# A power-of-two scale of V from a matmul of ones, and 26 groups of matmuls of ones ahead of the first layer product, in an attention, SoLU and bilinear kernel

## The chip, the cores and the metric

The kernel runs on one core of one Trainium2 chip. The metric is the device time of one execution in microseconds (us). Engine names: PE is TensorE (matmuls; PEld its weight loads), DVE is VectorE, ACT is ScalarE, POOL is GpSimd, SP is SyncE, whose queue issues all of the kernel's DMAs.

## The reference

Three layers follow each other. All inputs are float32 or float64 arrays made from a normal distribution.

```
# attention: q, k, v are [4, 8, 576, 64]
scores = q @ k.T / 8
mask   = heads 0..3: 0 <= i - j < 32;  heads 4..7: i >= j and i % 32 == j % 32
x      = softmax(where(mask, scores, -1e9)) @ v          # then [2304, 512]
# layer 1: w_in [512, 1024], w_out [1024, 512]
h  = x @ w_in
s  = h * softmax(h)
ln = (s - mean(s)) / sqrt(var(s) + 1e-6) * g_ln
y  = ln @ w_out
# layer 2: w_a, w_b [512, 1536], w_out2 [1536, 512]
out = ((y @ w_a) * (y @ w_b)) @ w_out2
```

Values that a half-precision matmul multiplies are split into a high and a low part, so that three products (high by high, high by low, low by high) carry the precision. Before such a split a tensor is scaled by a power of two, and the result is scaled back. For V this power comes from the largest magnitude in V; any power near it serves.

## The kernel before, in words

**The program is a list of steps.** Every piece of work is recorded with `pe(...)`, `dve(...)`, `act(...)`, `pool(...)` or `dma(...)` as a step with a key, a planned cost, and the buffers that it reads and writes. The first number of such a call is a planned cost; it only served to make the order. The order itself stands in the file as the list `ISSUE` (L60): 3261 step numbers, in which the steps are emitted. Each engine executes its own steps in that order and waits, where a step's data or buffer is not ready, with everything behind it in its queue waiting too. SP's queue issues the DMAs in the same way. Buffers come from rings of a fixed size: a new use of a buffer waits until the last use of the one before it is done.

**Attention.** The four batches are worked on one after the other (`attention`, L965 and on). In each there are four groups of two heads: two groups of strided heads (4 to 7), then two of local heads (0 to 3). `load_qk` and `load_v` fetch them. `group_T` (L600 to L618) transposes q and k with float32 matmuls against the identity (L608) into a bank of the ring `s`, and ACT copies them out. `att_tile` then makes one tile of attention: mask and scores on PE (L696, L701), the maximum, the subtraction and the sum on DVE (L719, L728, L732), the exponential on ACT (L731), the division on POOL (L768, L777), a transpose of the weights, and the product with V into the bank `x` (L798 for batch 0, L803 to L805 for the others), which ACT copies into `xT` (L825). Batch 0 is *direct*: it multiplies in float32, needs no scale of V, and transposes its weights on PE (L764). In batches 1 to 3 V and the weights are split in two half-precision parts, and the weights are transposed by a DMA (L786).

**The scale of V.** For batches 1 to 3 `pair_scale` (L622) makes one scale for the two strided groups and one for the two local ones, six in all. DVE reduces each group's V to one maximum per partition (L630), which gives two columns `am`. `pow2_scale` (L495) then finds the largest of all: PE transposes the columns (L500), DVE takes the maximum of each row (L501), PE transposes the two results into one row (L505), DVE takes the maximum again (L506), masks all but the exponent and makes a power of two and its inverse (L511 to L513), PE spreads the two numbers over all partitions by a matmul with ones (L515), and DVE multiplies in the units (L516). The scratch for this is the right part of the PSUM bank `xbank`, whose left part is the buffer `x` of the attention results; both are rings of one buffer. The same function makes one scale for w_out (`scale_wout`) and, in other banks, three in layer 2.

**Layer 1** runs beside the attention, a tile of 128 tokens at a time (`moe1`): ACT casts `xT` to `xh` (L845), DVE makes the rest `xl` (L849), and PE multiplies with the two parts of w_in in 24 products of 512 columns (L856) into `h`, a ring of one buffer of two banks. DVE, ACT and POOL make ln from it, a DMA transposes it, and `s2` multiplies with w_out (L910) into `y`. The weights come as float64 in eight loads of 512 KB for w_in (`load_win`, L454), are turned into float32 by ACT and DVE (L455, L461, L465) and split by ACT and POOL (L474, L475); the loads go through three raw buffers, so a later one waits for the conversion of an earlier one.

**Layer 2** begins when the attention is done. Its matmuls are L1326 (products with w_a and w_b) and L1472 (with w_out2). Ahead of it stands the one place where the kernel already multiplies ones by ones: `prime` (L1086) marks four banks in this way.

The constants are made at the beginning: `constants_a` the identity, `constants_b` and `constants_c` the two masks, `constants_d` (L424) the tiles of ones, `ones` in float32 and `onesb` in bfloat16, and some small ones. In `ISSUE` they stand in the order a, b, d, c on POOL.

Of the kernel before, what the change touches and what calls it, by code (L numbers as in the profile page):

```python
# [8 lines left out]
F32 = mybir.dt.float32  # L9
# [43 lines left out]
PARAM = dict(back=12, first=40, early=(0,), seed=4, noise=0.1, direct=((0, 0), (0, 1)), stay=0.0, pf1=(),  # L53
# [222 lines left out]
def tile_banded_attention_solu_bilinear(  # L276
# [19 lines left out]
    def pe(us, fn, r, w, cols=60, mode=0): return P.op("PE", us, fn, r, w, cols, mode=mode)  # L296
# [1331 lines left out]
```

## Time and profile before

| | |
|---|---|
| median of the runs | 700.77 us (3 runs, 699.4 to 700.79) |
| the profiled execution's own time | 695.03 us |
| its span, first to last instruction | 693.3 us |
| PE busy | 664.4 us (96%) |
| DVE busy | 571.5 us (82%) |
| ACT busy | 447.2 us (65%) |
| POOL busy | 144.7 us (21%) |
| mean granted clock of PE | 0.994 |
| DMA moved | 109.68 MB, mean 158 GB/s |

The profile shows a single execution. Its busy times are sums over instructions, whose ends are modelled for matmuls, and a stretch can be read as busy although its instructions only follow each other at a lower clock. The granted clock of PE is a share of full speed: 0.5 is the lower of its two levels, 1.2 GHz, and 1.0 the upper, 2.4 GHz. In a row that names a wait, the instruction on the left stood still until the one on the right was done.

### The profile page before, as it was taken

Reading aid. Unit: us, or ns where it says so; the run is one execution under the profiler, and the core shown is the slowest. Engines: PE = TensorE matmul, PEld = TensorE weight load, DVE = VectorE, ACT = ScalarE, POOL = GpSimd, SP = SyncE. Lnnn points to the kernel's source line nnn. Section 1 sums busy time; section 2 is a strip of 40 time slices with the busy share of each in tenths; the row PEclk is TensorE's granted clock in tenths of the full one; section 3 lists DMA queues with packets and bytes.
Section 4 is the critical chain, followed back from the end, with each engine's and each line's share of the span. In section 5 each row is a group of like instructions: output and inputs, shape, how many; then the busy total and the mean of one; then the engine's idle time right before and its main releaser. Section 6 shows DMA issues by size and latency. Waiting matters only on the chain.

```text
span 693.3 us, 15572 instructions
## 1 busy us (share of the span) xinstructions
PE 664.4 (96%) x5991; PEld 498.8 (72%) x5991; DVE 571.5 (82%) x1238; ACT 447.2 (65%) x898; POOL 144.7 (21%) x268
## 2 busy tenths in 40 slices
PE   5987899999999999999999999999999999999997
PEld 4766677878787888886576676766767676775676
DVE  5789899789678644999999999799977989786576
ACT  3679868777767644986978787676543746434421
POOL 5544546536537432410000000000000000000000
PEclk9999899999999999999999999999999999999999
DMA  9999979999998434677254043653522304641023
GB/s 209 258 243 244 188 138 194 264 186 268 222 248 199 102 81 102 188 249 240 103 184 152 0 141 104 198 201 97 175 100 94 120 32 166 237 138 46 1 92 122
DMA packets 152650, 109.68 MB, mean 158 GB/s; under 512 B 101376, under 2 KB 131072, under 8 KB 152576
## 3 DMA queue, kind: packets, MB, share of 16 engines
q1 hardware_dynamic: 152576, 108.69, 60.4%
q8 instruction: 47, 0.77, 0.5%
q14 instruction: 27, 0.22, 0.1%
HBM read 65.41 MB, written 27.53 MB: 134 GB/s over the span
## 4 chain that ended last, share of the span: by engine, by line
PE 61%; DVE 8%; ACT 5%; issue 1%; POOL 0%; ACTq 0%; POOLq 0%
PE N L1326 17%; PE M L1326 13%; PE N L1472 9%; PE y L910 7%; PE M L1472 7%; PE h L856 6%; ACT y L1267 1%; DVE p L1423 1%; ACT w L1128 1%; DVE w L1132 1%; DVE y L1269 1%; DVE A L1415 1%; DVE A L1393 1%; DVE V L647 0%; ACT Z L1238 0%
## 5 line engine op out<-in xcount | busy, mean ns | idle before, releaser
L1326 PEld LDWEIGHTS <-w 128*128 128x128 f16 x1512 | 147.9, 98 | 91.7 <-issue 2.0
L1326 PE MATMUL N<-y,w 128*128 128x384 f16 x864 | 156.2, 326 | 0.7 <-ACT N L1333 0.7
L1472 PEld LDWEIGHTS <-p 128*128 128x128 f16 x1071 | 104.7, 98 | 20.4 <-issue 1.1
L1326 PE MATMUL M<-y,w 128*128 128x384 f16 x648 | 118.5, 326 | 0.8 <-ACT N L1333 0.8
L910 PE MATMUL y<-lnT,wout 128*128 128x256 f16 x864 | 101.4, 273 | 1.5 <-DMA lnT<-ln 0.8
L910 PEld LDWEIGHTS <-wout 128*128 128x128 f16 x864 | 82.0, 98 | 15.2 <-issue 4.1
L1418 ACT CAST p<-A 128x384 f16<-128x384 f32 x119 | 59.2, 512 | 40.1 <-DVE A L1393 22.6
L856 PE MATMUL h<-win,xh 128*128 128x512 f32 x288 | 79.8, 417 | 2.7 <-DVE wk L871 2.6
L1472 PE MATMUL N<-wo,p 128*128 128x256 f16 x612 | 77.7, 273 | 1.0 <-DVE yst L1488 1.0
L856 PEld LDWEIGHTS h<-win,xh 128*128 128x128 f32 x288 | 54.4, 198 | 14.4 <-DVE wk L871 3.3
L1423 DVE TENSOR_TENSOR p<-A,p 128x384 f16<-128x384 f32 x119 | 62.3, 552 | 2.7 <-ACT p L1418 2.7
L1472 PE MATMUL M<-wo,p 128*128 128x256 f16 x459 | 60.2, 273 | 0.0
L455 ACT ACTIVATE f64f<-raw 128x512 f32<-128x512 f32 x52 | 34.6, 674 | 11.2 <-DMA raw<-in_moe_w_in_dram 7.3
L856 PE MATMUL h<-win,xl 128*128 128x512 f32 x144 | 39.2, 394 | 0.0
L1415 DVE TENSOR_TENSOR A<-A 128x384 f32<-128x384 f32 x72 | 39.0, 553 | 0.2
L1488 DVE SCALAR_TENSOR_TENSOR ob<-M,osc,ob 128x256 f32<-128x256 f32 x63 | 27.8, 477 | 12.6 <-PE M L1472 11.1
L777 POOL TENSOR_TENSOR e<-e,r 128x324 f32<-128x324 f32 (+2 forms) x30 | 26.2, 881 | 50.0 <-DVE r L738 28.2
L861 DVE TENSOR_REDUCE st<-h 128x1 f32<-128x1024 f32 x18 | 22.0, 1220 | 17.2 <-PE h L856 17.1
L856 PEld LDWEIGHTS h<-win,xl 128*128 128x128 f32 x144 | 26.7, 188 | 5.9
L465 DVE SCALAR_TENSOR_TENSOR f64f<-f64f,raw 128x512 int32<-128x512 int32 x36 | 28.8, 804 | 2.3 <-ACT f64f L455 1.8
L1348 ACT COPY V<-M 128x384 f32<-128x384 f32 x36 | 17.0, 473 | 20.0 <-PE M L1326 19.9
L871 DVE SCALAR_TENSOR_TENSOR wk<-h,st,wk 128x1024 f32<-128x1024 f32 x18 | 23.0, 1279 | 7.8 <-POOL st L869 7.7
(191 smaller groups left out, 1207.0 us busy)
## 6 DMA issues: line engine op xcount, KB each, us to landing
raw<-in_moe_w_out_dram SPq DMA_DIRECT2D x20, 512.0 KB
o_scr<-ob SPq DMA_DIRECT2D x36, 256.0 KB
ob<-o_scr SPq DMA_DIRECT2D x30, 256.0 KB
raw<-in_moe_w_a_dram SPq DMA_DIRECT2D x12, 512.0 KB
raw<-in_moe_w_b_dram SPq DMA_DIRECT2D x12, 512.0 KB
y_scr<-y SPq DMA_DIRECT2D x14, 384.0 KB
y<-y_scr SPq DMA_DIRECT2D x14, 384.0 KB
y_scr<-ys SPq DMA_DIRECT2D x18, 256.0 KB
```

The costliest lines, as they stand in the source:

```text
L455: act(0.67, lambda: nc.scalar.activation(f(), raw()[:, :, 1].bitcast(F32), AF.Prelu, scale=2.0 ** -112, alpha=-2.0 ** 32), (raw,), (f,))
L465: dve(0.77, lambda: nc.vector.scalar_tensor_tensor(g().bitcast(I32), f().bitcast(I32), 3, raw()[:, :, 0], op0=ALU.logical_shift_left, op1= ...
L777: pool(0.1 + 1.2 * pl, lambda: nc.gpsimd.tensor_tensor(ev(), ev(), r()[:, :ng].unsqueeze(2).to_broadcast([128, ng, nk]), op=ALU.mult), (r, ...
L856: nc.tensor.matmul(h()[:, 512 * n:512 * n + 512], xs[xa]()[:, kk], win[wa][:, kk, 512 * n:512 * n + 512], start=(pi == 0 and kk == 0), sto ...
L871: dve(1.3, lambda: nc.vector.scalar_tensor_tensor(e(), h(), st()[:, 7:8], e(), op0=ALU.mult, op1=ALU.mult, accum_out=st()[:, 2:3]), (h, (s ...
L910: nc.tensor.matmul(y()[:, 256 * mi:256 * mi + 256], wout[:, kk, wa, 128 * m:128 * m + 128], lnT()[:, xa, kk], start=(pi == 0 and kk == 0), ...
L1326: nc.tensor.matmul(to()[:, :HB], w()[:, wa, a, kk], y7[b]()[:, xa, kk], start=first and pi == 0 and kk == 0, stop=pi == 2 and kk == 1, ski ...
L1415: dve(TD, lambda: nc.vector.tensor_tensor(to(), x(), y(), op=op), toks, (to,))
L1418: act(0.5, lambda: nc.scalar.copy(pu(0, a), x()), (x,), (pu.tok(0, a),))
L1423: dve(TD, lambda: nc.vector.tensor_tensor(pu(1, a), x(), pu(0, a), op=ALU.subtract), (x, pu.tok(0, a)), (pu.tok(1, a),))
L1472: nc.tensor.matmul(bk(i), pus[u](xa, a)[:, 128 * tt:128 * tt + 128], wo()[:, u, b, wa], start=a == A11 and u == 0 and pi == 0, stop=u == U ...
L1488: dve(0.475, lambda: nc.vector.scalar_tensor_tensor(dst(), bk(i), s(), dst(), op0=ALU.mult, op1=ALU.add), (src, osc), (obt(t, c),))
```

## The change

The change has three parts. The scale of V is now made from the sum of the maxima of all partitions in place of their maximum. Two accumulating matmuls with a 128x128 tile of ones add up the columns `am` over the partitions and leave the sum on every partition at once. DVE masks the exponent, and three DVE steps make the power, its inverse and the unit. The result lies in the buffer `x`, which now is the whole bank `xbank`; the ring `scp` is gone, and the scale of w_out takes a buffer of `x` too. Next, 26 groups of eight matmuls of ones by ones (128 columns, bfloat16) are recorded, with keys from 3.5 to 38.5, which write an `h` buffer that nothing reads. They are the steps 13 to 38 of the new list, so that all later numbers shift: the first load of w_in, 181 before, is 207 now. Last, the planned costs of PE's steps are a little higher (0.05 to 0.1 for most) and the list `ISSUE` is written anew, now with 3263 numbers. In it `constants_d` (number 4 in both) is emitted first on POOL.

```
-PARAM = dict(back=12, first=40, ...
+PARAM = dict(warm=tuple(3.5 + 1.4 * i for i in range(26)), scp="x", back=12, first=40, ...
...
 ISSUE = [int(n) for n in """
-10 0 13 11 14 5 2 15 16 1 12 6 18 17 21 8 35 19 9 20 7 4 22 414 37 430 3 771 787 36 39 38 40 43 41 42 181 187 23 66 44
...
+5 4 39 0 40 13 41 11 2 1 10 42 6 14 43 44 12 207 8 15 45 9 213 7 61 219 440 452 3 789 801 63 46 62 65 16 64 66 67 17
...
-    ring("psR", "x", None, F32, 1).fixed = lambda n: xbank[:, :352]
-    ring("psR", "scp", None, F32, 1).fixed = lambda n: xbank[:, 352:]
+    ring("psR", "x", None, F32, 1).fixed = lambda n: xbank
...
-        tp = bank(ps) if ps == "M" else rings[ps].new()
+        tp = bank(ps) if ps == "M" else rings[ps or pm["scp"]].new()
...
-        pow2_scale(am, (am,), len(gs), 0, sc, sc)
+        tp, m1 = rings["x"].new(), rings["m1"].new()
+
+        def total():
+            for i in range(len(gs)):
+                nc.tensor.matmul(tp()[:, :1], ones_sq, am()[:, i:i + 1], start=i == 0, stop=i == len(gs) - 1)
+        pe(0.3, total, (am, "small"), (tp,))
+        dve(0.15, lambda: nc.vector.tensor_scalar(m1().bitcast(I32), tp()[:, :1].bitcast(I32), 0x7F800000, None,
+                                                  op0=ALU.bitwise_and), (tp,), (m1,))
+
+        def powers():
+            up, down = sc()[:, 0:1], sc()[:, 1:2]
+            nc.vector.tensor_scalar(down, m1(), 2.0 ** -14, 2.0 ** -60, op0=ALU.mult, op1=ALU.max)
+            nc.vector.reciprocal(up, down)
+            nc.vector.tensor_scalar(down, down, 1.0 / PSCALE, None, op0=ALU.mult)
+        dve(0.4, powers, (m1,), (sc,))
...
+    spare = rings["h"].new() if pm["warm"] else None
+
+    def warm():
+        for i in range(8):
+            nc.tensor.matmul(spare()[:, 128 * (i % 4):128 * (i % 4) + 128], onesb, onesb, start=True, stop=True)
+    for at in pm["warm"]:
+        P.key = at
+        pe(0.48, warm, ("small",), (spare,), 1024)
     P.key = -1.0
     load_next()
```

From the two lists, by engine: on PE the groups of ones are among the first 58 steps, three of them ahead of the first transposes, and the first product of layer 1 is PE's 62nd step (the 36th without the groups; it was the 31st). On SP the eight loads of w_in stand at places 7, 9, 10, 20, 24, 30, 33 and 38 (before: 15, 16, 27, 28, 31, 37, 39 and 43).

## Rows read from the trace of the kernel before

**Rows 1.** The page, part 1: busy us, share of the span, instructions of each engine

```profile
PE 664.4 (96%) x5991; PEld 498.8 (72%) x5991; DVE 571.5 (82%) x1238; ACT 447.2 (65%) x898; POOL 144.7 (21%) x268
```

**Rows 2.** Busy time by stretch: stretch, its length, then each engine's busy us, PEclk, DMA

```profile
0.00:43.70 43.70, 32.07 (x405) 26.20 (x406) 30.66 (x76) 24.15 (x47) 23.59 (x43) 1.00 1.02 236
...
43.70:67.30 23.60, 20.12 (x223) 15.85 (x221) 21.01 (x38) 20.57 (x45) 9.13 (x17) 1.00 1.04 249
...
67.30:71.00 3.70, 3.56 (x9) 2.84 (x10) 3.67 (x11) 3.70 (x8) 2.15 (x6) 0.54 0.92 154
...
81.00:84.50 3.50, 3.28 (x40) 2.48 (x40) 3.43 (x9) 3.04 (x6) 1.54 (x5) 0.51 1.41 166
...
84.50:110.00 25.50, 24.40 (x420) 19.91 (x420) 24.17 (x55) 18.64 (x32) 12.94 (x17) 1.00 0.88 162
...
110.00:240.00 130.00, 126.48 (x1594) 102.92 (x1592) 105.37 (x216) 95.44 (x183) 66.93 (x125) 1.00 1.02 214
...
360.00:600.00 240.00, 239.29 (x1720) 168.10 (x1718) 217.47 (x495) 157.70 (x348) 0.00 (x0) 1.00 0.40 134
```

**Rows 3.** Costliest groups of PE, by shape, 0 to 46.8 us (busy us, mean ns)

```profile
L608 PE MATMUL s<-ident,rawq 96*128 96x96 f32 x30 | 6.0, 374 | 4.2 <-DMA rawq<-in_q_dram 4.2
...
L856 PE MATMUL h<-win,xh 128*128 128x512 f32 x7 | 3.3, 642 | 0.0
```

**Rows 4.** The same groups of PE from 47 to 67 us

```profile
L608 PE MATMUL s<-ident,rawq 96*128 96x96 f32 x12 | 1.4, 255 | 0.0
...
L856 PE MATMUL h<-win,xh 128*128 128x512 f32 x26 | 6.9, 402 | 0.5 <-DVE wk L871 0.5
```

**Rows 5.** Timeline around the first product and a later one (start us, us, engine)

```profile
42.60 0.62 ACT L845 CAST xh<-xT 128x512 fp32r<-128x512 f32 x1
...
43.39 0.62 ACT L474 CAST win<-f64f 128x512 fp32r<-128x512 f32 x1 [0.16 <-DVE f64f L465]
...
43.80 3.52 PE L856 MATMUL h<-win,xh 128*128 128x512 f32 x8
...
48.06 1.98 PE L856 MATMUL h<-win,xh 128*128 128x512 f32 x8
...
67.44 3.64 PE L856 MATMUL h<-win,xh 128*128 128x512 f32 x8 [1.97 <-DVE wk L871]
```

**Rows 6.** Waits of DVE and ACT, 0 to 47 us (total us, times, longest)

```profile
DVE mx L719 <- PE s L701: 4.5, 2, 3.1
...
DVE raw L461 <- DMA raw<-in_moe_w_in_dram: 3.7, 3, 2.9
...
ACT f64f L455 <- DMA raw<-in_moe_w_in_dram: 7.3, 5, 2.6
```

**Rows 7.** Timeline: matmuls of ones that the kernel already has, in phase two

```profile
294.25 0.61 PE L1086 MATMUL N<-onesb 128*128 128x128 bf16 x8
```

**Rows 8.** The scale's VectorE steps, by line (duration ns min/median/max, first and last start us)

```profile
L501 DVE TENSOR_REDUCE m<-xbank x7: 238/270/279, 72.9 to 184.5; 2x1 f32<-2x128 f32 x6, 8x1 f32<-8x128 f32 x1
...
L506 DVE TENSOR_REDUCE m<-xbank x7: 115/146/154, 73.7 to 187.8; 1x1 f32<-1x2 f32 x6, 1x1 f32<-1x8 f32 x1
...
L511 DVE TENSOR_SCALAR m<-m x7: 109/141/142, 73.9 to 188.0; 1x1 int32<-1x1 int32 x7
...
L512 DVE TENSOR_SCALAR row<-m x7: 141/142/144, 74.0 to 188.2; 1x1 f32<-1x1 f32 x7
...
L513 DVE RECIPROCAL row<-row x7: 150/151/153, 74.2 to 188.3; 1x1 f32<-1x1 f32 x7
...
L516 DVE TENSOR_TENSOR sc<-xbank,units x6: 113/140/159, 85.2 to 215.1; 128x2 f32<-128x2 f32 x6
```

**Rows 9.** Waits of PE over the span, those on the scale's steps

```profile
PE xbank L505 <- DVE m L501: 1.1, 2, 0.7
...
PE xbank L500 <- DVE sc L516: 1.0, 2, 0.5
...
PE xbank L803 <- DVE sc L516: 1.0, 2, 0.6
```

More of the change, by code (lines that the diff above doesn't have):

```diff
@@ L51 @@
 PASSES = ((0, 0), (0, 1), (1, 0))
-PARAM = dict(back=12, first=40, early=(0,), seed=4, noise=0.1, direct=((0, 0), (0, 1)), stay=0.0, pf1=(),
+PARAM = dict(warm=tuple(3.5 + 1.4 * i for i in range(26)), scp="x", back=12, first=40, early=(0,), seed=4, noise=0.1, direct=((0, 0), (0, 1)), stay=0.0, pf1=(),
              pf2=(), ph1=(), pv=(), pp=(8,), ps1=(), ps2=(), ps3=False, ps4=False, passes=200, ysub=False, wsum=False, osum=False, plo2=(), so=(0, 1, 2), bM=8, bN=4, e=3,
@@ L493, in load_wout, with pow2_scale @@
             ("g", ("wof", c)), (f, ("wam", c)))
-    def pow2_scale(am, toks, n, unit, dst, dtok, top=14, least=60, ps="scp", sm=""):
-        tp = bank(ps) if ps == "M" else rings[ps].new()
+    def pow2_scale(am, toks, n, unit, dst, dtok, top=14, least=60, ps=None, sm=""):
+        tp = bank(ps) if ps == "M" else rings[ps or pm["scp"]].new()
         m1, row = rings[sm + "m1"].new(), rings[sm + "row"].new()
-        pe(0.12, lambda: nc.tensor.transpose(tp()[:n, :128], am(), ident), (*toks, "ident"), (tp,))
+        pe(0.2, lambda: nc.tensor.transpose(tp()[:n, :128], am(), ident), (*toks, "ident"), (tp,))
         dve(0.27, lambda: nc.vector.tensor_reduce(m1()[:n], tp()[:n, :128], axis=AX.X, op=ALU.max), (tp,), (m1,))
@@ L514, in pow2_scale @@
         dve(0.47, chain, (), (m2, row))
-        pe(0.1, lambda: nc.tensor.matmul(tp()[:, 144:146], ones, row()[:1], start=True, stop=True), (row, "small"), (tp,))
+        pe(0.25, lambda: nc.tensor.matmul(tp()[:, 144:146], ones, row()[:1], start=True, stop=True), (row, "small"), (tp,))
         dve(0.16, lambda: nc.vector.tensor_tensor(dst(), tp()[:, 144:146], units[:, unit], op=ALU.mult), (tp, "small"), (dtok,))
@@ L608, in transposes @@
                     nc.tensor.transpose(to, raw()[:, 128 * m:128 * m + 128], ident[:QT, :QT])
-            pe(NM * 0.09, transposes, ((raw, 0), (raw, 1), "ident"), (tp,), 855)
+            pe(NM * 0.09 + 0.05, transposes, ((raw, 0), (raw, 1), "ident"), (tp,), 855)
             def evac(c=c, tp=tp):
@@ L704, in att_tile @@
         if not (g.strided and j):
-            pe(2 * npb * nk * 0.42e-3 + sum(4 * kk / 2.4e3 + 0.01 for kk in groups) + 0.03, scores,
+            pe(2 * npb * nk * 0.42e-3 + sum(4 * kk / 2.4e3 + 0.01 for kk in groups) + 0.1, scores,
                ((g.T, 0), (g.T, 1), "identb", "masks" if g.strided else "maskl"), [(sp, f) for f in range(2)],
@@ L769, in att_tile @@
                                                            op=ALU.mult), (r, *ee), (e,))
-            pe(nblk * 0.14, transposes, (tok, "ident"), (pt,), nblk * rows * 2)
+            pe(nblk * 0.15 + 0.05, transposes, (tok, "ident"), (pt,), nblk * rows * 2)
             def evac():
@@ L806, in att_tile @@
         if direct:
-            pe(sum(4 * c[5] / 2.4e3 + (0.06 if g.strided else 0.015) for c in cells if not c[0]), pv, (PT, *g.vtoks), (x,),
+            pe(sum(4 * c[5] / 2.4e3 + (0.06 if g.strided else 0.015) for c in cells if not c[0]) + 0.07, pv, (PT, *g.vtoks), (x,),
                1.3 * sum(2 * c[5] * nk / 128 for c in cells), 1)
         else:
-            pe(sum(3 * c[5] / 2.4e3 + (0.035 if g.strided else 0.015) for c in cells if not c[0]), pv, (PT, *g.V), (x,),
+            pe(sum(3 * c[5] / 2.4e3 + (0.035 if g.strided else 0.015) for c in cells if not c[0]) + 0.07, pv, (PT, *g.V), (x,),
                1.27 * sum(1.5 * c[5] * nk / 128 for c in cells), 1)
@@ L858, in mm @@
                                          start=(pi == 0 and kk == 0), stop=(pi == 2 and kk == 3))
-                s1_ops.append(pe(4 * 0.230, mm, [xs[xa]] + [((("win", kk, n), wa)) for kk in range(4)], (h,), 2048))
+                s1_ops.append(pe(4 * 0.237, mm, [xs[xa]] + [((("win", kk, n), wa)) for kk in range(4)], (h,), 2048))
         st, e, ln = rings["st"].new(), rings["wk"].new(), rings["ln"].new()
@@ L928, in scale_ab @@
         x, y = wab[:, u, 0, m:m + 1], wab[:, u, 1, m:m + 1]
-        pe(0.12, lambda: nc.tensor.matmul(tp()[:, :2], ones_sq, fro[:, u, m], start=True, stop=True),
+        pe(0.22, lambda: nc.tensor.matmul(tp()[:, :2], ones_sq, fro[:, u, m], start=True, stop=True),
            [("fro", u, m, i) for i in range(2)] + ["small"], (tp,), 8)
```

262 rows, old and new, of the table ISSUE are left out of this document.

## The prediction, made before the changed kernel was run

> **What bounds the kernel now.** I read the page's engine shares first, then busy time by stretch, then the shapes of TensorE (PE) at the head, then who waits there. PE is busy 96% of the span [rows 1]: 28.9 us of 693.3 are left. By stretch the picture splits. From 110 us on PE is the limit: 126.5 of 130 us, and 239.3 of 240 us later. Before that it isn't: of the first 43.7 us it is busy 32.1, and from 43.7 to 110 VectorE (DVE) is the fullest engine, 21.0 of 23.6 us at first and 24.2 of 25.5 us at the end of it [rows 2]. So what can be won lies ahead of 110 us, and what is won there arrives at the end, since PE behind it runs without gaps.
>
> Part of PE's busy time at the head is no work. The granted clock reads 1.00 from 0 to 43.7 us, but the durations speak against it: the same transposes of q take 374 ns before 46.8 us and 255 ns after 47 us, the same products of the first layer 642 and 402 ns [rows 3, 4]. The first eight products take 3.52 us, eight others 1.98 us, and eight more 3.64 us at a moment for which the granted clock is 0.54 over the stretch [rows 2, 5]. I read it so: until about 47 us the clock stands on its lower level (1.2 of 2.4 GHz), and the column shows a default where nothing was recorded. It falls there twice more, in the stretches with 0.54 and 0.51 [rows 2]; ahead of the first of these PE had sat idle for 1.97 us, waiting for DVE [rows 5]. Work costs 3.52 / 1.98 = 1.78 times as much on that level.
>
> **The change, part by part.** Durations are of the profiled execution: span 693.3 us, its own time 695.03. The median of the runs, 700.77, is 5.74 us above that; I forecast the change against 695.03 and put it on the median, which assumes that this gap stays.
>
> *Groups of ones.* 26 groups of eight 128-column matmuls enter PE's queue ahead of the first product. Eight such cost 0.61 us on the upper level [rows 7], the drain of the last included, so 26 cost 15.9 us; on the lower level, times 1.78, 28.2 us. The head's own work is 32.1 us now and 32.1 / 1.78 = 18.0 us on the upper level. If the groups raise the clock early, PE has 18.0 + 15.9 = 33.9 us to do within a head of 43.7: about what it does today, with each real step shorter. The groups read only a tile of ones and write a buffer of h that nobody reads, so no other engine waits for them; what stands behind them in PE's queue does, each time up to 0.61 us. The constants' memsets are moved to the front of GpSimd's queue for them (one step of some ten small memsets, now behind the masks), so the first groups fill PE's first idle time, before q has landed (4.2 us [rows 3]).
>
> What a faster PE gives the head is not 32.1 - 18.0 us, since it waits for others. The first product starts at 43.80; its x is cast at 42.60, and the last part of the weights w_in is cast at 43.39, as late [rows 5]. DVE waited for scores of PE for 4.5 us, but 3.1 of these are a single wait near the beginning, where the clock may not be up; ScalarE (ACT) waited 7.3 us and DVE 3.7 us for the loads of w_in [rows 6]. The DMA engines are full through all of it (share 1.02 [rows 2]). The new order puts the first three w_in loads seventh, ninth and tenth in SP's queue instead of fifteenth, sixteenth and twenty-seventh, ahead of q and k of the second pair of heads, which are then late by as much; and it runs the scores of batch 1 ahead of the first product, where PE now runs six steps of products among them. Bounds for the head, with the clock up: nothing (DMA sets its length anyway), and 7.3 + 4.5 / 2 = 9.5 us (every wait for w_in goes, and half of that for scores). I take **-3.5 us**, nearer to nothing, as full DMA engines speak for that end.
>
> *First tile of products.* Eight products at 1.98 instead of 3.52 us: **-1.5 us**, and nothing if the clock isn't up by then.
>
> *The two later falls.* The first costs 3.64 - 1.98 = 1.7 us, the second 3.28 x (1 - 1 / 1.78) = 1.4 us of PE's time [rows 2, 5]. No group of ones stands there, but the order around them is another. Bounds 0 and -3.1 us; I take half, **-1.5 us**.
>
> *Scale of V.* Six pairs of heads have one (batches 1 to 3). Now it goes to PE three times (two transposes, one spread by ones) with DVE between; afterwards once, two accumulating matmuls of a column each. On DVE, 0.270 + 0.146 + 0.141 + 0.142 + 0.151 + 0.140 = 0.99 us [rows 8] become the mask and three column steps, 0.141 + 0.142 + 0.151 + 0.142 = 0.58 us by the same rows: 6 x 0.41 = 2.5 us less. PE sat idle 1.1 + 1.0 + 1.0 = 3.1 us on these steps [rows 9]. The new matmul writes the bank x, whose one buffer is that of the attention results: it waits until ACT has copied the result before it, and the next result waits in PE's queue until DVE has read the sum. That wait is there already, in the last of these rows (L803, which writes x, behind L516), because the old scratch lies in the same bank. Bounds: all 3.1 us gained, or 2 us lost (a longer such wait in a full DVE queue, as long as twice the 1.0 us of a row). Idle PE and a full DVE overlap, so I take **-1.5 us**.
>
> *The order written out.* Every queue is re-ordered, most up to the middle of the program and hardly at its end. Before 110 us that is in the terms above. Behind it PE has no gaps to win, only some to lose: 0, with 3 us either way, near the 3.5 us that PE idles from 110 to 240 us [rows 2].
>
> Sum: 3.5 + 1.5 + 1.5 + 1.5 = 8.0 us; 687.0 against 695.03, **692.8 us** against the median.
>
> **Rivals.** *The clock stays down and the groups are only load (slower).* Place: the head, in PE's queue ahead of the first product. Price: 32.1 + 28.2 = 60.3 us of PE work where the first product now starts at 43.8, so it starts 16 us later or more; PE's idle time from 43.7 to 110 us can take back some 5 us and the scale 1.5: about +9.5, 710 us. It decides from where the groups no longer fit: with the clock up after x us and PE at work from about 1.3 us on, x / 1.78 + (42.4 - x) must reach 33.9, so x below some 19 us. For it: PE is busy 73% of the head now and the clock doesn't rise. Against: it did rise within 4 us of the first products, and the groups stand densest at the beginning.
>
> *DMA and DVE set the pace anyway.* The head doesn't shrink, the later falls stay; 1.5 us of the first tile remain, and little of the scale: 699 us. For it: DMA share 1.02 and a DVE that is 95% busy behind the head.
>
> *The clock rises and falls again between the groups.* PE then spends half of the head on each level: (33.9 + 60.3) / 2 = 47 us of work, which doesn't fit in 43.7 and eats the gain on the first tile and the scale: 698 us with the order's better start left. The two falls after pauses of PE of some 2 us are rows that speak for it [rows 5]. The Trainium skill, "TensorE: Matmul & The Clock Gate", section "A second HAM failure mode: psum-queue depth-cycling", says that many small pauses between groups of matmuls make the clock swing between its levels, and that the repeated cold starts cost throughput. The trace agrees so far as it shows falls in a stretch of small attention matmuls, and none in the dense ones from 110 to 240 and from 360 to 600 us [rows 2].
>
> **How the numbers follow.** Forecast 0.62, load only 0.13, DMA and DVE 0.15, swinging clock 0.10. A measurement of this kernel can tell about 0.2% (1.4 us) from no change. The rival at 699 lies 1.8 us below, so half of it counts as no change: same 0.07, slower 0.13, faster 0.62 + 0.10 + 0.08 = 0.80. Range: low 685, the head at its full 9.5 us and part of the scale's bound; high 702, which takes in both rivals near 698 and the order's 3 us. Left out are the case of 710 and a gap between runs and profile that shrinks by much (if it too comes from the clock, the result is lower).
>
> **What would show it.** Right: L608 and L856 at about 255 and 402 ns from some 10 us on; the first product at about 40 us or, if it is later, with more of batch 1 done ahead of it; no or one stretch of low clock after 47 us; PE's waits on the scale below 1 us; 110 us reached some 6 to 8 us earlier in the order of work; nothing changed behind 240 us. Wrong: transposes at 370 ns still at 30 us (load only); SP's loads of w_in as late as now and DVE idle (DMA); long waits of PE on the new mask step (the shared bank).

## The result, and the profile after

The changed kernel took **705.07 us** (median of 8 runs, 702.51 to 709.77), the kernel before in the same comparison 699.61 (8 runs, 697.65 to 701.48): a ratio of **1.0079 [1.0050, 1.0108]**. It is 5.5 us slower. The forecast was 692.8 us and faster; the range ended at 702.

The profiled execution took 705.84 us, near its median. That of before took 695.03, 4.6 us under 699.6: in the 122 runs of the kernel before that stand beside the experiments it went from 694.47 to 704.68, and only one of them was as fast as 695.03. So 10.8 us between the two profiles is twice what the change costs, and no single pair of profiles gives its price.

First the page's part 1, to be held against [rows 1]:

```profile
PE 674.2 (96%) x6199; PEld 507.7 (72%) x6199; DVE 566.9 (81%) x1226; ACT 448.3 (64%) x898; POOL 150.5 (21%) x268
```

PE is busy 9.8 us more, with 208 more instructions; its share is 96% as before. DVE has 4.6 us less.

Busy time by stretch, as in [rows 2] (stretch, its length, busy us of each engine, PEclk, DMA share, GB/s); the three stretches with a clock of 0.50 or 0.51 are those that the trace's records of the granted clock give:

```profile
0.00:45.40 45.40, 38.37 (x684) 34.01 (x684) 30.25 (x81) 27.85 (x54) 25.69 (x46) 0.96 1.06 227
45.40:58.30 12.90, 9.63 (x112) 7.17 (x112) 10.74 (x24) 9.56 (x22) 3.34 (x4) 1.00 1.01 222
58.30:68.50 10.20, 8.85 (x60) 6.93 (x59) 8.92 (x19) 8.69 (x18) 5.12 (x10) 0.50 0.89 191
75.30:82.20 6.90, 5.88 (x32) 4.02 (x33) 5.69 (x15) 3.02 (x6) 3.18 (x8) 0.51 1.30 221
92.40:99.20 6.80, 6.75 (x52) 5.38 (x50) 6.73 (x15) 6.80 (x12) 3.58 (x5) 0.50 0.94 133
110.00:240.00 130.00, 127.49 (x1535) 104.70 (x1530) 100.26 (x195) 91.97 (x171) 64.95 (x121) 1.00 0.98 211
...
360.00:600.00 240.00, 238.13 (x1706) 166.58 (x1704) 217.11 (x495) 158.07 (x347) 0.00 (x0) 1.00 0.37 124
```

The clock did what the forecast hoped for at the head: the first record of the full clock is at 10.5 us, with one fall of 3.4 us at 34.4. The shapes agree. From 10.5 to 34.4 us (busy us, mean ns) the transposes of q take 250 ns, as after 47 us in [rows 4], not the 374 of [rows 3]:

```profile
L1002 PE MATMUL h<-onesb 128*128 128x128 bf16 x123 | 8.6, 221 | 1.9 <-issue 1.9
...
L607 PE MATMUL s<-ident,rawq 96*128 96x96 f32 x18 | 2.0, 250 | 0.0
```

But the first product starts at 45.44 us, not 43.80 [rows 5]. Five more steps of attention stand ahead of it on PE in the new order, four of transposes and one of scores, so this alone doesn't show whether the head gained. What follows is worse. The timeline of PE, with the idle time before an instruction and what ended it:

```profile
45.44 2.14 PE L869 MATMUL h<-win,xh 128*128 128x512 f32 x8
...
53.39 0.69 PE L607 MATMUL s<-ident,rawq 96*128 96x96 f32 x6 [0.92 <-DMA rawq<-in_q_dram]
...
57.77 0.73 PE L607 MATMUL s<-ident,rawk 96*128 96x96 f32 x6 [2.14 <-DMA rawk<-in_k_dram]
...
61.85 1.20 PE L607 MATMUL s<-ident,rawq 96*128 96x96 f32 x6 [1.35 <-DMA rawq<-in_q_dram]
...
63.39 3.78 PE L869 MATMUL h<-win,xh 128*128 128x512 f32 x8
...
68.61 2.00 PE L869 MATMUL h<-win,xh 128*128 128x512 f32 x8
```

The eight products at 45.44 are fast, then batch 1's transposes, which the new order has placed among the first tile's products, wait three times for q or k. The clock falls at 58.3 us, and the next tile's first eight products take 3.78 us, more than the 3.52 of [rows 5]. After 45 us the clock is low for 23.9 us in three stretches, in the profile of before for 6.8 in two. Nothing is recorded there until 46.9 us; by the 3.52 us of its first eight products [rows 5] the stretch from 45 to 46.9 was low too, which makes it 8.7.

The waits of DVE and ACT, 0 to 47 us, against [rows 6]:

```profile
DVE raw L460 <- DMA raw<-in_moe_w_in_dram: 5.6, 2, 5.1
...
ACT f64f L454 <- DMA raw<-in_moe_w_in_dram: 4.2, 4, 2.9
...
DVE mx L732 <- PE s L714: 2.7, 3, 1.9
```

Those of PE over the span, against [rows 9]:

```profile
PE s L607 <- DMA rawq<-in_q_dram: 3.0, 3, 1.4
PE s L607 <- DMA rawk<-in_k_dram: 2.1, 1, 2.1
...
PE xbank L818 <- DVE V L660: 1.4, 1, 1.4
PE y L923 <- DVE sc L643: 1.2, 1, 1.2
```

ACT's wait for w_in fell from 7.3 to 4.2 us, but DVE's rose from 3.7 to 5.6, 5.1 of it in one wait that ends at 10.5 us. The wait on PE's scores, 4.5 us before, is 2.7. The transposes wait 5.1 us for q and k together, 4.4 of it behind 47 us; before it was one wait of 4.2 us, for the first q [rows 3]. Of the waits in [rows 9] none is left in this form. One of 1.2 us is put down to the scale's last step (L643), but the instruction that waits, L923, doesn't read the scale, so what it waited for is open; 1.4 us go to the scaled V. The scale stands as written; its last column step has the duration of the steps in [rows 8]:

```profile
L643 DVE TENSOR_SCALAR sc<-m x6: 135/148/154, 86.4 to 224.9; 128x1 f32<-128x1 f32 x6
```

A second loss lies where nothing was forecast, at the start of the second layer. The same view of busy time by stretch there:

```profile
310.00:330.00 20.00, 20.00 (x156) 15.12 (x155) 10.78 (x21) 9.47 (x18) 3.14 (x2) 1.00 0.78 268
330.00:370.00 40.00, 36.87 (x253) 24.06 (x251) 39.52 (x84) 31.25 (x62) 0.00 (x0) 1.00 0.43 148
```

What DVE waited for from 300 to 330 us (total us, times, longest):

```profile
DVE A L1358 <- PE N L1347: 4.4, 2, 4.0
DVE S L1218 <- DMA yst<-w_scr: 3.1, 2, 1.9
DVE wo L1232 <- ACT wo L1228: 1.3, 1, 1.3
```

What PE waited for from 325 to 380 us:

```profile
PE M L1347 <- ACT N L1354: 1.0, 1, 1.0
PE M L1347 <- ACT y L1288: 0.8, 1, 0.8
PE N L1347 <- DVE A L1358: 0.7, 1, 0.7
PE M L1347 <- DVE y L1290: 0.6, 1, 0.6
```

The steps named here are sums over the output weights (L1218), their low parts (L1232) and the first combination of PE's results (L1358). DVE stands idle 9.2 of 20 us; then it is full for 40 us, and PE, which had no wait above 1 us there in the old order, waits 3.1 us in four places for DVE and ACT.

### The profile page after: what moved, and what is told of

Its sections match the earlier page's. It is cut to its first block, busy times and chain, and to the rows that moved or that the text cites. A ratio compares the mean times of both kernels' runs of the same rounds, so it can differ in the third digit from the quotient of the medians.

```text
span 704.1 us, 15967 instructions
## 1 busy us (share of the span) xinstructions
PE 674.2 (96%) x6199; PEld 507.7 (72%) x6199; DVE 566.9 (81%) x1226; ACT 448.3 (64%) x898; POOL 150.5 (21%) x268
## 4 chain that ended last, share of the span: by engine, by line
PE 49%; DVE 20%; ACT 3%; issue 2%; DMA 2%; POOL 1%; SPq 0%; DVEq 0%; ACTq 0%; POOLq 0%
PE N L1347 12%; PE M L1347 9%; PE N L1493 7%; PE y L923 7%; PE h L869 6%; PE M L1493 5%; DVE p L1444 3%; DVE w L1153 2%; DVE y L1290 2%; DVE S L1139 1%; DVE A L1436 1%; DVE A L1414 1%; DVE ob L1509 1%; DVE C L1358 1%; DMA raw<-in_moe_w_out_dram 1%
## 5 line engine op out<-in xcount | busy, mean ns | idle before, releaser
L923 PE MATMUL y<-lnT,wout 128*128 128x256 f16 x864 | 100.1, 273 | 1.6 <-DVE sc L643 1.2
L923 PEld LDWEIGHTS <-wout 128*128 128x128 f16 x864 | 82.5, 98 | 14.8 <-issue 4.6
L869 PE MATMUL h<-win,xh 128*128 128x512 f32 x288 | 81.4, 422 | 2.2 <-DVE wk L884 2.0
L869 PE MATMUL h<-win,xl 128*128 128x512 f32 x144 | 41.8, 414 | 0.0
L1509 DVE SCALAR_TENSOR_TENSOR ob<-N,osc,ob 128x256 f32<-128x256 f32 x45 | 20.5, 481 | 14.3 <-PE N L1493 13.7
L798 POOL TENSOR_TENSOR P<-e,P 128x324 f16<-128x324 f32 (+2 forms) x30 | 28.1, 942 | 10.1 <-ACT P L797 10.0
```

The source lines that it names most:

```text
L798: pool(0.15 + 1.4 * pl, lambda: nc.gpsimd.tensor_tensor(plo, ev(), ph, op=ALU.subtract), (e, ("P2", pi, 0)), (("P2", pi, 1),))
L869: nc.tensor.matmul(h()[:, 512 * n:512 * n + 512], xs[xa]()[:, kk], win[wa][:, kk, 512 * n:512 * n + 512], start=(pi == 0 and kk == 0), sto ...
L923: nc.tensor.matmul(y()[:, 256 * mi:256 * mi + 256], wout[:, kk, wa, 128 * m:128 * m + 128], lnT()[:, xa, kk], start=(pi == 0 and kk == 0), ...
L1509: dve(0.475, lambda: nc.vector.scalar_tensor_tensor(dst(), bk(i), s(), dst(), op0=ALU.mult, op1=ALU.add), (src, osc), (obt(t, c),))
```

## The experiments

The theories at the outset: **A**, the order written anew is the loss; **B**, the groups are (by their load, or by a clock that swings later); **C**, the scale is, through the ring it now shares. Every kernel was timed against before on the same chip; the ratio is given with its 95% interval. It isn't the ratio of the two medians, and the two can differ. Kernels that ran beside different runs of before are compared by these ratios; a difference of two is uncertain by some 0.35%, or 2.5 us.

### One part at a time: four kernels

`old_order_groups` is before with the groups, put ahead of the same PE steps as in the changed kernel, and GpSimd's constants first:

```
-PARAM = dict(back=12,
+PARAM = dict(warm=tuple(3.5 + 1.4 * i for i in range(26)), back=12,
...
+    for at in pm["warm"]:
+        P.key = at
+        pe(0.48, warm, ("small",), (spare,), 1024)
```

> The order of the kernel before, with the 26 groups of ones put ahead of the same PE steps as in the changed kernel (those that would stand behind the first product, just ahead of it) and the tiles of ones made first; scale of V as before. Theory A (the loss is in the order written anew: batch 1's transposes wait for q and k with the products of the first layer behind them in PE's queue, PE pauses and the clock falls): the groups alone lose nothing, the clock rises near 10 us, the first tile of products runs at full clock; 695 to 699 us against 699.6 before. Theory B (the groups are what costs, as load or through a clock that swings): 703 us or more, and stretches of low clock behind 47 us of some 20 us in sum.

Measured: 701.69 us, **1.0027 [1.0004, 1.0049]**, between the two ranges. The clock rose at 4.9 us, as A said, but the low clock behind 47 us sums to 20.5 us, B's sign. The sum proves little: in profiles without groups it ranges from 12.8 to 24.1 us behind 45 us.

`old_order_sum_scale` is before with the sum scale alone, in the scratch columns of the bank that the scale had before:

```
-        pow2_scale(am, (am,), len(gs), 0, sc, sc)
+        tp, m1 = rings["scp"].new(), rings["m1"].new()
+
+        def total():
...
```

> The order of the kernel before, no groups; the scale of V by the sum of the maxima, its three steps at the places of the first transpose, of the first and of the second maximum of before, in the scratch columns of before. Theory A: 698 to 700 us, PE's waits on the scale below 1.5 us instead of 3.1, nothing worse. Theory C (the scale costs: longer waits on the shared bank): 702 us or more.

Measured: 697.64 us, **0.9977 [0.9946, 1.0008]**. No wait of PE on the scale's steps stands in its profile.

`new_order_no_groups` is the changed kernel without the groups:

```
-PARAM = dict(warm=tuple(3.5 + 1.4 * i for i in range(26)), scp="x", back=12,
+PARAM = dict(warm=(), scp="x", back=12,
```

> The changed kernel without the 26 groups, all else in its order. Theory A: as slow as the changed kernel or slower, 704 to 712 us, with the clock on its lower level through the head (transposes of q near 370 ns until some 47 us) and the same waits of PE for q and k of batch 1. Theory B: 700 us or less.

Measured: 702.77 us, **1.0037 [1.0011, 1.0064]**, below A's 704 and above B's 700.

`old_order_both` is before with groups and sum scale:

> The order of the kernel before with both, the groups of ones and the sum of the maxima. Theory A: faster than before, 694 to 698 us. Theories B and C: 703 us or more.

Measured: 699.78 us, **0.9973 [0.9943, 1.0002]**, again between the ranges. Its runs lie apart, four at 694.6 to 695.4 and eight at 698.0 to 702.4, and the medians would give 1.0002.

What follows: with the scale and without groups, the new order costs 1.0037 - 0.9977 = 0.6%, about 4.2 us by the ratios. The scale is no loss. The groups gained nothing in either pair: 0.27% lost in one, nothing in the other (0.3% in both, by medians). So A holds for the order as the larger loss; that the groups alone lose nothing, which A said too, isn't borne out. The next question was where in the order.

### Which stretch of the order

Here one list is followed up to a place, and the rest is in the other list's order. All three have the sum scale in columns of its own and no groups. A1 is the wait of batch 1's transposes at the head, A2 the start of the second layer, A3 what lies between.

`first_stage_new`: the first 610 of 3237 steps from the new order, up to the first product of the fifth tile, the rest as before.

> The new order up to the first product of the fifth tile of the attention stage (109 us in the run of the new order without groups), the order of before from there on; sum scale, no groups. Against the old order with the sum scale (697.64) the whole new order cost 5.1 us by medians. Theory A1, the loss lies where batch 1's transposes wait for q and k ahead of the first products: 701 to 703, all or nearly all of the 5 us. Theory A2, the loss lies in the start of the second layer, where VectorE is idle half of 310 to 330 us and the queue of products then waits: 696 to 699, with the products of the second layer spaced as before (some 32.6, 32.2 and 26.4 us from one 126 to the next). Theory A3, the stage between (109 to 287 us): also 696 to 699, and the run of the new order up to the second layer tells A2 from A3.

Measured: 702.91 us, **1.0029 [1.0008, 1.0051]**. By itself this is what A1 asked for. But at that place the two orders differ by 43 steps, and the switch makes a wait that neither has (waits of PE, 95 to 130 us):

```profile
PE xbank L636 <- DVE am L629: 2.7, 1, 2.7
```

`first_layer_new`: 1329 steps from the new order, up to the sixteenth tile's first product. There the two orders differ by one step.

> The new order up to the first product of the sixteenth tile (263.7 us in the run of the new order without groups), the order of before from there on; sum scale, no groups. A1 and A3: 701 to 703. A2: 697 to 699, and VectorE is busy 18 of the 20 us from 310 to 330, not 11.

Measured: 699.55 us, **0.9989 [0.9968, 1.0011]**, against 0.9972 for the old order (the mean of two runs of the sum scale alone). A1 and A3 asked for 701 to 703. So the new head and the rest of the new first layer together cost some 1 us, if anything. What batch 1's transposes wait for q and k can't be priced from one profile: in the four kernels with this head and no groups these waits sum to 0 (here), 1.2 (`new_order_no_groups`), 2.4 (`first_stage_new`) and 4.0 us (`new_order_own_columns`).

`second_layer_new`: 1328 steps as before, the rest new.

> The order of before up to the first product of the sixteenth tile, the new one from there on; sum scale, no groups. A1 and A3: 697 to 699. A2: 700.5 to 702.5, VectorE busy 10 to 12 us of the 20 from 310 to 330, and 36 us, not 32, between the second and the third 126 products of the second layer.

Measured: 700.59 us, **1.0001 [0.9976, 1.0027]**, 0.29% or 2 us over the old order, which by itself isn't clear of the noise. Busy time by stretch in the old order (`old_order_sum_scale`):

```profile
310.00:330.00 20.00, 20.00 (x147) 14.01 (x145) 18.86 (x39) 13.70 (x26) 1.15 (x1) 1.00 0.71 235
330.00:370.00 40.00, 39.14 (x276) 26.63 (x274) 39.59 (x89) 32.43 (x65) 0.00 (x0) 1.00 0.43 154
```

The same in `first_layer_new`:

```profile
310.00:330.00 20.00, 20.00 (x145) 13.79 (x144) 18.86 (x40) 13.69 (x26) 0.38 (x1) 1.00 0.70 228
330.00:370.00 40.00, 39.18 (x278) 26.84 (x277) 39.59 (x88) 33.13 (x67) 0.00 (x0) 1.00 0.42 152
```

The same in `second_layer_new`:

```profile
310.00:330.00 20.00, 20.00 (x155) 14.61 (x153) 10.72 (x25) 9.69 (x19) 0.00 (x0) 1.00 0.53 174
330.00:370.00 40.00, 36.86 (x259) 24.92 (x258) 39.59 (x85) 32.45 (x65) 0.00 (x0) 1.00 0.46 162
```

In the first two DVE is busy 18.9 us of the first 20, in the third 10.7, and then PE is busy 2.3 us less of 40. The waits of PE from 325 to 380 us in the old order:

```profile
PE M L1339 <- ACT N L1346: 0.9, 1, 0.9
```

And in `second_layer_new`:

```profile
PE M L1339 <- ACT N L1346: 1.0, 1, 1.0
PE M L1339 <- ACT y L1280: 0.8, 1, 0.8
PE N L1339 <- DVE A L1350: 0.7, 1, 0.7
PE M L1339 <- DVE y L1282: 0.6, 1, 0.6
```

A2 is right in place, in DVE's idle time and in the 36 us from the second to the third 126 products of this layer (333.9 to 370.1 us). In the profiles it reached the sixteenth tile 2.7 us ahead of the old order (260.4 against 263.1), and the last 126 products level with it (644.3 against 644.5).

The profiles price this stretch better than the times do, since the falls of the clock at the beginning are left out. From the first product of the sixteenth tile to the last of the second layer's first products (L1339 here) the nine kernels with the old order there take 411.9 to 413.2 us, the five with the new one 414.7 to 416.3: 2.8 us by the means, without overlap.

### Twice the groups

`double_groups` has 52 groups in the old order:

```
-PARAM = dict(warm=tuple(3.5 + 1.4 * i for i in range(26)), back=12,
+PARAM = dict(warm=tuple(3.5 + 1.4 * i for i in range(52)), back=12,
```

> The order of before, sum scale, and 52 groups of matmuls of ones in place of 26, each standing twice at its place, all ahead of the layer's first product. With none it took 697.64, with 26 699.78. If the groups cost their own time on TensorE's queue in the head (theory B1): 701 to 703, with the first product some 2 us later than with 26. If TensorE's spare time in the head covers them and the 2 us are later falls of the clock that more work ahead brings on (B2): 699 to 702 with the head as long as with 26 and the clock's full stretch starting by 10 us. If the 26 cost nothing and the 2 us were chance (B3): 697 to 699.

Measured: 700.55 us, **0.9991 [0.9966, 1.0016]**, B2's number but not B2's reason. The first three tiles of products in PE's timeline, without groups (`old_order_sum_scale`):

```profile
44.02 3.70 PE L869 MATMUL h<-win,xh 128*128 128x512 f32 x8
...
60.46 3.78 PE L869 MATMUL h<-win,xh 128*128 128x512 f32 x8
...
72.80 2.11 PE L869 MATMUL h<-win,xh 128*128 128x512 f32 x8 [1.97 <-DVE wk L884]
```

With 52 groups:

```profile
50.97 2.06 PE L871 MATMUL h<-win,xh 128*128 128x512 f32 x8
...
61.84 2.14 PE L871 MATMUL h<-win,xh 128*128 128x512 f32 x8 [0.78 <-DVE wk L886]
...
72.28 3.05 PE L871 MATMUL h<-win,xh 128*128 128x512 f32 x8 [1.97 <-DVE wk L886]
```

And with 26 (`old_order_both`):

```profile
45.18 2.09 PE L870 MATMUL h<-win,xh 128*128 128x512 f32 x8
...
60.27 3.78 PE L870 MATMUL h<-win,xh 128*128 128x512 f32 x8
...
72.58 2.11 PE L870 MATMUL h<-win,xh 128*128 128x512 f32 x8 [1.97 <-DVE wk L885]
```

All other steps stand in one order in the three, but for the tiles of ones, which are made first where there are groups. The first product comes at 44.0, 45.2 and 51.0 us, the third tile at 72.8, 72.6 and 72.3. So the groups made the first eight products faster (3.70 to 2.1 us) and delayed them, and two tiles later nothing was left of either: PE's queue doesn't set the pace here. The third tile waits 1.97 us for DVE's `wk` in all three, as it does in [rows 5].

### The shared ring, the groups again, the gain again

`change_own_columns` is the whole change with the scratch columns as a ring of their own:

```
-    ring("psR", "x", None, F32, 1).fixed = lambda n: xbank
+    ring("psR", "x", None, F32, 1).fixed = lambda n: xbank[:, :352]
+    ring("psR", "scp", None, F32, 1).fixed = lambda n: xbank[:, 352:]
...
-        tp, m1 = rings["x"].new(), rings["m1"].new()
+        tp, m1 = rings["scp"].new(), rings["m1"].new()
```

> The whole change, but the scales keep the scratch columns of the PSUM bank that they had before, as a ring of their own, in place of sharing the ring of the attention's sums. If the shared ring costs (C1): 1.003 to 1.006 of before, against 1.0079 for the change as it is. If it costs nothing (C2): 1.007 to 1.009.

Measured: 704.04 us, **1.0055 [1.0029, 1.0080]**, in C1's range. `new_order_own_columns` is the same without the groups:

> The new order throughout, sum scale with columns of its own, no groups. C1: 1.001 to 1.002 of before, as the two halves of the order measured singly add up to (1.0012 and 1.0024 over the old order with the sum scale, 0.9977). C2: 1.003 to 1.004, as with the shared ring (1.0037).

Measured: 703.20 us, **1.0052 [1.0027, 1.0078]**, above what either theory said. Own columns made one pair 0.24% faster and the other 0.15% slower: the ring costs nothing that can be measured, and C falls. The two stretches measured singly, 0.17% and 0.29% over the old order, do not add up to the 0.65 to 0.80% of the order as a whole; within their uncertainty they could.

`change_old_second_layer` is `change_own_columns` with the order of before from the sixteenth tile on:

> The whole change with groups, its order up to the first product of the sixteenth tile and the order of before from there on, scales with columns of their own. If second layer and ring cost what the halves say (2 to 3 us of lost order, up to 1.5 us of ring): 0.999 to 1.003 of before, TensorE waiting under 1.2 us from 325 to 380, not 3.1. If the groups are the loss in this order, whatever comes later: 1.004 to 1.007. Against the same kernel without groups (0.9989) it gives the price of the groups in the new head: 2 to 3 us, if the clock's later falls among the products are what they cost; nothing, if the head's transfers cover them.

Measured: 701.44 us, **1.0017 [0.9991, 1.0042]**. The order from the sixteenth tile on is worth 0.38% here and 0.63% without groups (0.9989 against 1.0052), 2.7 and 4.4 us, each uncertain by 2.5 us; the profiles' 2.8 us fits both. Against 0.9989 the groups cost 0.28%, within the noise. PE waits 0.9 us from 325 to 380, as in the old order.

`sum_scale_again` repeats the kernel with the sum scale alone:

> The order of before without groups, with the sum scale alone, run again: the one edit of the change that seemed to gain. 0.9977 with an interval that took in 1 before; if the gain of some 2 us on VectorE's path is real, 0.996 to 0.999 again, and the two together leave 1 out; else 0.999 to 1.002.

Measured: 697.59 us, **0.9967 [0.9947, 0.9987]**. The scale gains about 2 us. It is the fastest kernel of the study, ahead of both that were given.

### Within the second layer's stretch

`old_from_second_products` follows the new order for 1503 steps, up to the second layer's first product, and `old_from_second_126` for 1627, up to its 127th.

> The new order up to the first product of the second layer (303 to 306 us), the order of before from there on; sum scale with columns of its own, no groups. The new order throughout took 1.0052 of before (1.0037 with the shared ring), with the old order from the sixteenth tile on 0.9989. If VectorE's work is brought forward already ahead of the first product, so that it runs dry at 311 us whatever follows (D1): 1.003 to 1.005, VectorE busy 11 to 14 of the 20 us from 310 to 330 and TensorE waiting 2 us or more from 325 to 380. If the loss lies in the order behind that product (D2): 0.998 to 1.001, VectorE busy 18 of 20.

Measured: 705.45 us, **1.0098 [1.0071, 1.0124]**, more than D1's 1.003 to 1.005. DVE is busy 9.4 us of the 20, still less than D1's 11 to 14, and PE waits 0.7 us from 325 to 380, not 2. Its wait is another, for the transposed `lnT`, and is paid before 325 us. PE's timeline:

```profile
311.75 6.93 PE L923 MATMUL y<-lnT,wout 128*128 128x256 f16 x48 [3.32 <-DMA lnT<-ln]
```

Busy time by stretch:

```profile
310.00:330.00 20.00, 18.25 (x135) 13.98 (x136) 9.40 (x20) 6.75 (x13) 2.24 (x2) 0.91 0.77 264
```

The switch thus adds a loss of its own, 3.3 us and a fall of the clock behind it, and its time can't be taken as the price of D1; its dry DVE can be taken as a sign, part of which is PE's delay (DVE waited 5.9 us for PE and 3.0 for the loads).

> The new order up to the 127th product of the second layer (337 us), the order of before from there on; sum scale with columns of its own, no groups. VectorE is idle from 311 to 330 as in the new order. If that idle time is what is lost (D1 and D2 both): 1.003 to 1.005. If TensorE loses it only by the order in which the second tile's rescaling stands on VectorE and ScalarE from 337 us on (D3): 0.998 to 1.001, and TensorE waits 1 us from 325 to 380, not 3.1.

Measured: 703.54 us, **1.0054 [1.0031, 1.0078]**. Busy time by stretch:

```profile
310.00:330.00 20.00, 20.00 (x157) 15.09 (x155) 10.89 (x21) 9.47 (x18) 3.14 (x2) 1.00 0.84 276
```

The whole loss is there although the order behind 337 us is that of before, and PE waits 2.8 us from 325 to 380. D3 falls. With `first_layer_new`, which follows the old order from the sixteenth tile and loses little, this puts the cause between 263 and 337 us. In that stretch the new order has brought forward work of DVE that the old one leaves for later: when the first product of the second layer is issued, four low parts of weights, a set of sums and two pairs of steps that convert float64 weights have gone out that the old order has still to come. Their planned costs in the file sum to 7.7 us; in the profiles DVE is busy 8.1 us less from 310 to 330 (18.9 against 10.7). So DVE has nothing left while the loads of the output weights (`w_scr`) and PE's first results are under way. That this is the work which is missed is read from the lists and the waits; no kernel moved those steps alone, so the place of the loss is shown and these steps as its cause are argued.

## Why the prediction was wrong

**Two steps failed, and the miss needs both.** The forecast change was -8.0 us, the measured one +5.5. The terms of the head, of the first tile and of the later falls, -6.5 us, all rest on one step: a clock raised by the groups shortens the way to 110 us. The groups came out at about +1.3 us. And "The order written out", put at "0, with 3 us either way", came out at 4 to 5.6 us. Added to the forecast one at a time, the first gives 700.6 us, the second 697 to 698.4; only together do they reach the measured time to within 1 or 2 us.

**The order.** It cost 0.6 to 0.8% with the scale in and the groups out. The largest part known, 2.8 us by the profiles, lies from the sixteenth tile on and shows at the start of the second layer. The prediction passed over it because the order differs "hardly at its end" and PE has no gaps there; none of its rows covers 240 to 360 us. PE's lack of gaps was the wrong comfort. DVE is 217 of 240 us busy behind it [rows 2], and in the old order 58 of the 60 us from 310 to 370. In the changed kernel DVE stood idle for 9 us up to 330, and PE's waits of 3.1 us came from 348 to 363. What the rest of the order costs, 1 to 3 us by the difference, isn't located.

**Head, "-3.5 us": not gained.** Its clock part was right, the first full clock at 10.5 us and transposes of 250 ns. But the bound "nothing (DMA sets its length anyway)" was nearest: with 0, 26 and 52 groups in one order the first product came later each time and the third tile at the same time. The rival "DMA and DVE set the pace anyway" comes closest to this. For DVE the same wait for `wk` in all three speaks; that the loads set the pace is read from the waits for w_in, and no kernel changed the loads. That rival's 699 us lacked the order's loss.

**First tile, "-1.5 us": gained in eight products, lost in the tile.** They took 2.14 us for 3.52, but the tile with its transposes took 12.0 us from first product to DVE's first maximum (45.4 to 57.4). It took 8.1 in the profile of before (43.8 to 51.9), 11.2 and 10.3 in the two of the old order with the scale alone. The sign asked for, 110 us reached 6 to 8 us earlier, stayed out: the fifth tile's first product came at 112.6 us, before at 110.4.

**The later falls, "-1.5 us": the wrong sign.** Low clock after 45 us was 23.9 us in this profile; it was 16.4 and 20.5 in the new order without groups, and 18.6 and 12.8 in the old order with the scale alone. The profile of before had 8.7, the least of all, and the prediction took half of its two falls as to be won. It also read both as falls after pauses of some 2 us. [Rows 5] show one; ahead of the second, at 81.0 us, the longest wait was 1.2 us. The rival "clock rises and falls again between the groups" had its falls in the wrong place: one of 3.4 us among the groups, the rest among the products, and these come without groups as well. The rule that I cited there, the Trainium skill, "TensorE: Matmul & The Clock Gate", section "A second HAM failure mode: psum-queue depth-cycling", has many small pauses swing the clock; the trace agrees in so far as the stretch from 45.4 to 58.3 us, PE busy 9.6 of 12.9 us, ends in a fall.

**Scale, "-1.5 us": right.** Two comparisons gave 0.23% and 0.33%, 1.6 and 2.3 us, and PE's waits on its steps are gone. The loss feared from the shared bank was not seen.

**Groups.** Their price was put inside the head's term. Six pairs of kernels with and without them (52 against none among them) differ by +0.27, -0.04, +0.19, +0.42, +0.03 and +0.28%: no gain, on the average 0.19% or 1.3 us lost (by medians all six are losses, 0.12 to 0.43%). Only the first pair, measured directly against before, and narrowly the fourth, the changed kernel with and without them, have an interval that leaves out 0. The rival "load only" needed a clock that stays down, and it rose; its 710 us is not what happened. Why they cost anything is open.

**The gap, "assumes that this gap stays".** It didn't: the profile after lies 0.8 us over its median. The profile of before was an unusually fast execution, with a lead of 2.6 and 3.8 us over the two of the old order with the scale alone from the third tile on (DVE's first maximum at 76.8 us, there 79.4 and 80.6). It has the least low clock, but that this was the reason isn't shown: among the 122 runs the eleven with a mean granted clock of 0.99 or more (it counts a beginning without records as full) have a median of 700.4 us.

One reading was wrong without weight: from 84.5 to 110 us PE is the fullest engine, not DVE, 24.4 against 24.2 us [rows 2].

By ratios: scale -0.28%, order +0.65 to +0.80%, groups +0.19% make +0.56 to +0.71%; measured +0.79% [0.50, 1.08].

## What to carry to other kernels

A faster engine helps only where a wait on it ends last: here raising TensorE's clock at the head changed the durations and not the time at which the third tile could start, which waited for VectorE. When an order is written anew, compare the queues of every engine over the whole program, not TensorE's gaps: where work of a nearly full engine is brought forward, look whether it runs dry later; here the waits that followed came tens of microseconds after. And before a gain is put on a profile, see whether that execution is an ordinary one; here it was 4.6 us faster than its median.

## What was not expected of the hardware

The clock's rises and falls are not fixed by the kernel. By the traces' records two profiles of the same kernel (`old_order_sum_scale`, `sum_scale_again`) had the clock low from 37.3 to 47.5, 57.8 to 64.6 and 85.1 to 88.5 us in one, and from 19.3 to 46.6, 56.8 to 63.6, 84.1 to 90.9 and 125.1 to 128.5 in the other. Without groups it can be full at 15.8 us too, for 3.4 us. And one pause in a dense stretch went with a fall: in `old_from_second_products` PE waited 3.3 us for `lnT` until 311.75 us, the clock read low from 311.5 to 314.9, and 16 products of 256 columns there took 409 ns each, against 273 ns for the same shape in the changed kernel's page.
